# Second chunk of a Fourier-mixing kernel: half of it by plain sums, half by seven products

## The chip, the cores and the metric

One core of one Trainium2 chip. The metric is the device time of one execution in microseconds (us), as the median of several runs. The engines are named as in the profile: PE is TensorE's matmul, PEld its weight load, DVE VectorE, ACT ScalarE, POOL GpSimd, SP SyncE, whose queue issues most of the DMAs.

## The reference

`x` has 2048 tokens of 512 values, all in float32. Of its normalized rows a two-dimensional Fourier transform is taken (real part) and multiplied by a gate from a two-layer network:

```
xn = layernorm(x)
a  = xn @ hid_re.T ;  b = xn @ hid_im.T                # 2048 x 512
s  = seq_re @ a - seq_im @ b                           # 2048 x 2048 matrices
h  = relu(xn @ w1 + b1)**2                             # 2048 x 1792
out = x + s * silu(h @ w2 + b2)
```

The kernel takes the transform along the sequence first, `PQ = [seq_im; seq_re] @ xn`, and the one along the hidden dimension after it.

## The kernel before, in words

**Operands.** Each float32 operand is split into a HI and a LO part (`split`: a copy with rounding on ACT, `split_hi`, line 136, and a subtraction on DVE, `split_lo`, line 139). A product is three matmul passes, HI x HI, HI x LO and LO x HI (`PASSES`).

**The sequence transform.** Its output is cut into `NC` = 8 chunks of `CW` = 256 rows. The sum over 2048 tokens is cut into `NJ` = 8 pairs `j` (128 tokens of the first half of the sequence and 128 of the second). `XC[j]` holds pair j of xn as the stationary operand, in seven slots of two parts: the four raw quarters A11, A21, A12, A22 and the sums S1 to S4, where S1 shares a slot with A21. The slots are HI and LO parts of what lies in `xn32`, which shares buffers `wd0` and `wd1` with the prepared weights. A step (c, j) loads a 512 KB frame `u` of the Fourier matrix (three buffers), forms four more quarters of it (`step_sums`: three DVE operations, lines 304 to 306), splits seven quarters into an operand `g` (`step_split`; two buffers, `ga` for even j and `gb` for odd j) and multiplies.

- *Plain* chunks (0 and 1, `PLAIN` = 2): each pair takes 24 matmuls of 128 x 512 (`one_product`, line 397), into four PSUM banks (`accs`). Only the raw quarters are split, 1024 columns (`plain_parts`). Chunk 0 is accompanied by the layer norm.
- *Seven-product* chunks (2 to 7): Strassen-Winograd products, 7 x 6 = 42 matmuls of 128 x 256 a step (`mm`, line 382), into seven banks, `ms[k]`. The chunk's four quarters are combined from the seven banks at its end (`closing_of`: copies on ACT, seven DVE operations), two of them at once and the rest spread over the next chunk's steps by the table `LATER`, then stored to `PQD[c]` in DRAM.

**Work beside chunk 1.** A chain `aside` is drawn on while chunk 1's products run, with a budget a step (`beside`): `sums(g)` forms S1 to S4 of four pairs in four DVE operations of 1024 columns, S1 in a tile of its own; `split_sums(j)` splits S2 to S4 into `XC[j]`, `split_s1(j)` splits S1 after pair j's last plain product; then the jobs `d0` and `d1`. The frame of chunk 2's first steps is prepared at its end.

**The weights' jobs.** `weight` is a generator of four stages: load the raw weight; form sums (DVE, and for `d` one ACT copy); split and store three slots; split and store four. `d0` to `d3` make the hidden transform's weights (`WDD`), `v0`, `v1`, `v6` three of w1's. They use buffer `pq00`/`pq01` for raw and sums and `wd0` or `wd1` for the parts. The table `EARLY` names after which step which job advances by one stage; `p` loads prepared weights back, `y` prepares what follows.

**Order.** Everything is in program order on each engine, written out by hand. In each iteration of the loop over `steps`: the products of step n, `step_sums(n + 2)`, `step_split(n + 1)`, `step_load(n + 4)`, closing operations, and the jobs of `EARLY`.

**Afterwards.** The hidden transform (`YUnit`, lines 790 on) and the first layer (`HUnit`, 28 units) run as units of seven products; a unit's stages c11, c22, c21, c12 and square run in the midst of the next unit. For units in `ACT_PAIR` both lower quarters get their relu and square on ACT (lines 848 and 879), with plain DVE operations before (lines 800 and 803); for others DVE adds the bias and does relu and square of the lower quarters (lines 860 and 875) and ACT squares half as much. Each unit's region B starts as a negated copy of A (`seed`, line 794). The second layer (`outer`, line 896) ends the kernel.

Of the kernel before, what the change touches and what calls it, by code (L numbers as in the profile page):

```python
# [11 lines left out]
ALU = mybir.AluOpType  # L12
# [10 lines left out]
PLAIN = 2  # L23

ASIDE = 3.6

SIDE = {7: 1}
# [22 lines left out]
LATER = {0: 1, 1: 1, 2: 2, 4: 1}  # L50

# [43 lines left out]
ACT_PAIR = (4, 5, 6, 8, 10, 12, 14, 16, 18, 21, 25)  # L95
# [9 lines left out]
A11, A21, A12, A22, S2, S3, S4 = range(7)  # L105
S1 = A21

# [23 lines left out]
def fnet_gated_kernel(ctx, tc, x, xt, ct, wd, w1, w2, b1, b2, out):  # L131
# [122 lines left out]

    def ln_hi(j, h):

        nc.vector.tensor_scalar(XC[j][:, 2 * h:2 * h + 2, HI, :], halves(xr[j][:, h]), stats[:, 0, h, j:j + 1],
                                stats[:, 1, h, j:j + 1], op0=ALU.subtract, op1=ALU.mult)

    def xc_parts(j, h):  # L260
        s = slice(2 * h, 2 * h + 2)
        return XC[j][:, s, HI, :], XC[j][:, s, LO, :], halves(xn32[j][:, h])

    s1 = {}

    def sums(g):


        s = xn32[ND * g, "tile"].rearrange("p j h (b n) -> p j (h b) n", b=2)
        t = s1[g] = buf(f"pq1{g}", [P, ND, CW], f"s1_{g}")  # L270
        for to, a, b, op in ((t, s[:, :, 1], s[:, :, 3], ALU.subtract),
                             (s[:, :, 1], s[:, :, 1], s[:, :, 0], ALU.subtract),
                             (s[:, :, 0], t, s[:, :, 0], ALU.subtract),
                             (s[:, :, 2], s[:, :, 2], s[:, :, 0], ALU.add)):
            nc.vector.tensor_tensor(to, a, b, op=op)
            yield 1.2

    def split_sums(j):
        s = xn32[j].rearrange("p h (b n) -> p (h b) n", b=2)
        split(XC[j][:, S2:S4 + 1, HI, :], XC[j][:, S2:S4 + 1, LO, :], s[:, 0:3])  # L280
        return 0.9

    def split_s1(j):
        split(XC[j][:, S1, HI, :], XC[j][:, S1, LO, :], s1[j // ND][:, j % ND])
        return 0.4
# [9 lines left out]
    def plain_parts(c, j, hs=slice(0, 2)):  # L295
        if (c, j) not in part:
            part[c, j] = operand_buf("g" + "ab"[j % 2], f"g{c}_{j}", 0 if (c, j) == (PLAIN - 1, NJ - 1) else 3 if j in TURNED else 1, (2, 4, CW))
# [57 lines left out]
    def closing_of(part_, ms, room):  # L355
# [4 lines left out]
        for to, m, frm, op in ((C11, 2, C21, ALU.add), (C22, 6, C21, ALU.add), (C21, 7, C22, ALU.subtract),  # L360
                               (C12, 5, C22, ALU.subtract), (C22, 5, C21, ALU.add), (C12, 3, C12, ALU.add),
                               (C21, 4, C21, ALU.subtract)):
# [10 lines left out]
    def some(steps_, n):  # L373
        for _ in range(n):
            next(steps_)

# [9 lines left out]
    accs = [[bank(tag, f"pq0_{tag}") for tag in ("b20", "b21", "bb", "bc")]]  # L386

    def products(c, j, h):

        for passes in [PASSES] if c else [[q] for q in PASSES]:  # L390
            for k in range(ND):
                one_product(c, j, h, k, passes)

    def one_product(c, j, h, k, passes=PASSES):
        for a_, b_ in passes:
            w = XC[j][:, 2 * h + k // 2, a_, k % 2 * P:(k % 2 + 1) * P]
            nc.tensor.matmul(accs[c][k], w, part[c, j][:, b_, 2 * h:2 * h + 2],  # L397
                             start=j == 0 and h == 0 and (a_, b_) == (HI, HI),
# [832 lines left out]
```

## Time and profile before

| | us |
|---|---|
| median of 3 runs (lowest to highest) | 673.12 (672.95 to 673.25) |
| the profiled execution, its own time | 672.81 |
| its span, first to last instruction | 671.0 |
| PE busy | 665.1 |
| DVE busy | 596.4 |
| ACT busy | 380.2 |
| chunk 1's first matmul starts | 50.95 |
| chunk 2's first matmul starts | 94.67 |
| the hidden transform's first matmul starts | 323.16 |

Times in the profile count from the span's start. Rows in order of time read: start, duration, engine, line, operation, output <- inputs, shapes, count, and in brackets the engine's idle time before it with what ended it. Rows by group have count, busy time, mean duration in ns, idle time before them. A duration is longer than the distance to the next start where operations overlap in an engine's pipeline.

### The profile page before, as it was taken

The page shows a single profiled execution, that of the slowest core. Times are in us where ns is not written, and L with a number is a line of the kernel's source. Part 1 is how long each engine was busy: PE and PEld are TensorE (multiplying, and loading weights), DVE is VectorE, ACT ScalarE, POOL GpSimd, SP SyncE. Part 2 cuts the span into 40 slices and gives each one's busy share as a digit, 9 for nine tenths or more (in the row PEclk, how much of TensorE's full clock was granted, in tenths as well). Part 3 has the DMA queues.
Part 4 walks back from the last instruction along what each step waited for, and adds up shares of the span by engine and source line. Part 5 has one row for each costly group of instructions (what it writes and reads, how often), then busy time and mean ns, then how long its engine had stood idle before and what let it go on. Part 6 is the DMA issues. An engine that isn't in the chain of part 4 may idle for free.

```text
span 671.0 us, 13184 instructions
## 1 busy us (share of the span) xinstructions
PE 665.1 (99%) x5437; PEld 646.3 (96%) x5437; DVE 596.4 (89%) x831; ACT 380.2 (57%) x524; POOL 8.8 (1%) x11
## 2 busy tenths in 40 slices
PE   9999999999999999999999999999999999999997
PEld 6888889999999999999999999999999999999997
DVE  7997888999999999899899988977877889999997
ACT  6855664634445454444464557888778865454451
POOL 0000000000000000000000000000000000101010
PEclk9999999999999999999999999999999999999999
DMA  8635497646556774759588558565755866777775
GB/s 292 226 115 206 145 347 269 220 142 224 200 167 226 252 282 162 262 186 346 184 303 278 181 189 317 202 251 205 271 182 198 324 243 214 190 218 190 219 205 156
DMA packets 51739, 150.82 MB, mean 225 GB/s; under 512 B 4960, under 2 KB 19552, under 8 KB 50272
## 3 DMA queue, kind: packets, MB, share of 16 engines
q1 hardware_dynamic: 43568, 129.28, 56.9%
q10 hardware_dynamic: 6208, 18.88, 7.1%
q0 software_dynamic: 1904, 1.84, 1.9%
q8 instruction: 42, 0.69, 0.4%
q14 instruction: 17, 0.14, 0.1%
HBM read 101.98 MB, written 47.99 MB: 223 GB/s over the span
## 4 chain that ended last, share of the span: by engine, by line
PE 96%; DVE 1%; ACT 1%; DMA 0%; issue 0%; ACTq 0%; SPq 0%; DVEq 0%
PE m L382 34%; PE m_o L896 15%; PE r_B L790 13%; PE r_A L790 9%; PE pq_b L397 8%; PE r_C L790 4%; PE r_D L790 4%; PE m_last L896 4%; PE pq_ba L397 2%; PE pq_bc L397 2%; PE pq_bb L397 2%; DVE z L1146 0%; DMA x<-in_x 0%; DVE z L946 0%; ACT h L848 0%
## 5 line engine op out<-in xcount | busy, mean ns | idle before, releaser
L382 PEld LDWEIGHTS m<-g,xc 128*128 128x128 f32 x2016 | 228.6, 188 | 0.1
L382 PE MATMUL m<-g,xc 128*128 128x256 f32 x2016 | 228.7, 276 | 0.0
L136 ACT ACTIVATE g<-u 128x1792 fp32r<-128x1792 f32 (+2 forms) x65 | 99.0, 1523 | 126.9 <-PE m L382 89.0
L139 DVE TENSOR_TENSOR g<-u,g 128x1792 fp32r<-128x1792 f32 (+2 forms) x66 | 116.9, 1772 | 19.8 <-ACT g L136 19.2
L896 PE MATMUL m_o<-w,g 128*128 128x256 f32 x882 | 100.5, 276 | 0.0
L896 PEld LDWEIGHTS m_o<-w,g 128*128 128x128 f32 x882 | 100.3, 188 | 0.0
L136 ACT ACTIVATE g<-hr 128x1792 fp32r<-128x1792 f32 (+2 forms) x31 | 48.2, 1565 | 40.0 <-PE m_o L896 16.8
L790 PE MATMUL r_B<-xT,w 128*128 128x256 f32 x504 | 66.6, 277 | 0.4 <-ACT r_B L146 0.4
L397 PE MATMUL pq_b<-g,xc 128*128 128x512 f32 x240 | 65.2, 391 | 0.4 <-DVE small L247 0.4
L790 PEld LDWEIGHTS r_B<-xT,w 128*128 128x128 f32 x504 | 61.5, 188 | 0.5 <-ACT r_B L146 0.5
L139 DVE TENSOR_TENSOR g<-hr,g 128x1792 fp32r<-128x1792 f32 (+2 forms) x31 | 56.7, 1837 | 2.9 <-ACT g L136 2.8
L397 PEld LDWEIGHTS pq_b<-g,xc 128*128 128x128 f32 x240 | 44.7, 188 | 10.7 <-ACT g L136 0.8
L790 PE MATMUL r_A<-xT,w 128*128 128x256 f32 x336 | 42.8, 276 | 0.0
L790 PEld LDWEIGHTS r_A<-xT,w 128*128 128x128 f32 x336 | 40.2, 188 | 0.0
L790 PE MATMUL r_B<-wdp,yg 128*128 128x256 f32 x288 | 35.8, 277 | 0.0
L304 DVE TENSOR_TENSOR u<-u 128x512 f32<-128x512 f32 x48 | 32.8, 684 | 1.9 <-DMA u<-in_ct 1.9
L790 PEld LDWEIGHTS r_B<-wdp,yg 128*128 128x128 f32 x288 | 34.1, 188 | 0.0
L896 PE MATMUL m_last<-w,g 128*128 128x256 f32 x294 | 33.5, 276 | 0.0
L896 PEld LDWEIGHTS m_last<-w,g 128*128 128x128 f32 x294 | 33.4, 188 | 0.0
L139 DVE TENSOR_TENSOR yg<-yraw,yg 128x1792 fp32r<-128x1792 f32 x13 | 26.2, 2018 | 0.6 <-ACT yg L136 0.6
L136 ACT ACTIVATE yg<-yraw 128x1792 fp32r<-128x1792 f32 x13 | 22.2, 1708 | 5.8 <-DVE yraw L313 5.3
L790 PE MATMUL r_D<-xT,w 128*128 128x256 f32 x168 | 23.6, 276 | 0.0
(192 smaller groups left out, 877.8 us busy)
## 6 DMA issues: line engine op xcount, KB each, us to landing
u<-in_ct SPq DMA_DIRECT2D x63, 512.0 KB, 3.8
hd<-h ACTq DMA_DIRECT2D x28, 512.0 KB, 3.9
hr<-hd SPq DMA_DIRECT2D x28, 512.0 KB, 3.8
wdp<-wdd SPq DMA_DIRECT2D x8, 896.0 KB, 6.5
yraw<-pqd SPq DMA_DIRECT2D x13, 512.0 KB, 5.9
pqd<-c SPq DMA_DIRECT2D x6, 1024.0 KB, 6.3
w<-w1d SPq DMA_DIRECT2D x6, 896.0 KB, 8.2
y<-y ACTq DMA_DIRECT2D x8, 512.0 KB, 5.2
```

The lines of the kernel that those rows point to most:

```text
L136: nc.scalar.activation(hi, src, AF.Copy)
L139: nc.vector.tensor_tensor(lo, src, hi.bitcast(F32), op=ALU.subtract)
L304: nc.vector.tensor_tensor(t[:, 0:2], r[:, 0:1].to_broadcast([P, 2, 256]), r[:, 1:3], op=ALU.add)
L382: nc.tensor.matmul(ps[:, d], w[:, a_, d * P:(d + 1) * P], halves(mv(b_)), start=first and d == 0 and (a_, b_) == (HI, HI), stop=last and ( ...
L397: nc.tensor.matmul(accs[c][k], w, part[c, j][:, b_, 2 * h:2 * h + 2], start=j == 0 and h == 0 and (a_, b_) == (HI, HI), stop=j == NJ - 1 a ...
L790: nc.tensor.matmul(self.region(REGION[k]), w, mv, start=i == 0 and k in (1, 7), stop=i == len(ops) - 1, skip_group_check=True)
L896: nc.tensor.matmul(m[:, i * 256:(i + 1) * 256], ready[n][:, a_, H_SLOT[a], i * P:(i + 1) * P], W2[p][:, b_, b], start=p == 0 and i == 0 an ...
```

## The change

Chunk 1 becomes mixed. It takes pairs 4 to 7 first (`MIXED`), plain, as four sums of 128 x 256 matmuls through `mm` (`plain_step`): three of the sums go into the banks of products 2, 4 and 3, the fourth into a bank `Z`. Then pairs 0 to 3 follow as seven-product steps into the same banks, as the first four entries of `steps`. Its closing has one DVE operation more where Z's quarter is added, and `LATER_1` spreads it. The slots of `XC` are in another order, so that S2, S3, S4 and S1 lie side by side: `sums` works in place, and `split_sums` splits all four in one operation of 1024 columns on each engine. The chain `aside` is gone: sums and splits stand at fixed places, and the jobs d0 and d1 move into `EARLY`, which shifts those behind them. d1 uses the same raw buffers as the others. Chunk 0's banks change, `junk` has another bank, `g` of chunk 1 has another address offset (`operand_buf`'s step 0), and unit 5 leaves `ACT_PAIR`. The core of the diff:

```diff
-PLAIN = 2
-ASIDE = 3.6
-SIDE = {7: 1}
+MIXED = 4, 5, 6, 7
 EARLY = {
-    (2, 0): ("d2",), (2, 1): ("d2",), (2, 2): ("d3",), (2, 4): ("d3",), (2, 5): ("d3",), (2, 6): ("d3",),
-    (3, 1): ("v0",), (3, 3): ("v0",), (3, 5): ("v0",), (3, 6): ("v0",),
-    (4, 1): ("v1",), (4, 3): ("v1",), (4, 5): ("v1",), (4, 6): ("v1",),
-    (5, 1): ("v6",), (5, 2): ("p1",), (5, 3): ("v6", "p1"), (5, 5): ("v6",), (5, 6): ("v6",),
-    (6, 1): ("y1",), (6, 3): ("y1", "p0"), (6, 6): ("p0",),
+    (1, 0): ("d0",), (1, 2): ("d0",), (1, 3): ("d0",), (2, 0): ("d0", "d1"), (2, 3): ("d1",), (2, 5): ("d1",),
+    (2, 6): ("d1", "d2"), (3, 0): ("d2",), (3, 1): ("d2",), (3, 3): ("d2", "d3"), (3, 5): ("d3",), (4, 0): ("d3",),
+    (4, 1): ("d3", "v0"), (4, 3): ("v0",), (4, 5): ("v0",), (4, 6): ("v0", "v1"), (5, 0): ("v1",), (5, 1): ("v1",),
+    (5, 2): ("p1",), (5, 3): ("v1", "v6", "p1"), (5, 5): ("v6",), (5, 6): ("v6",),
+    (6, 0): ("v6",), (6, 1): ("y1",), (6, 3): ("y1", "p0"), (6, 6): ("p0",),
...
 LATER = {0: 1, 1: 1, 2: 2, 4: 1}
+LATER_1 = {0: 1, 1: 1, 2: 2, 3: 1, 4: 1}
-ACT_PAIR = (4, 5, 6, 8, 10, 12, 14, 16, 18, 21, 25)
+ACT_PAIR = (4, 6, 8, 10, 12, 14, 16, 18, 21, 25)
-A11, A21, A12, A22, S2, S3, S4 = range(7)
+A11, A12, A22, S2, S3, S4, A21 = range(7)
 S1 = A21
...
-        for to, a, b, op in ((t, s[:, :, 1], s[:, :, 3], ALU.subtract),
...
+        for to, a, b, op in ((3, 1, 3, ALU.subtract), (1, 1, 0, ALU.subtract), (0, 3, 0, ALU.subtract), (2, 2, 0, ALU.add)):
+            nc.vector.tensor_tensor(s[:, :, to], s[:, :, a], s[:, :, b], op=op)
...
-        split(XC[j][:, S2:S4 + 1, HI, :], XC[j][:, S2:S4 + 1, LO, :], s[:, 0:3])
-    def split_s1(j):
-        split(XC[j][:, S1, HI, :], XC[j][:, S1, LO, :], s1[j // ND][:, j % ND])
+        split(XC[j][:, S2:S1 + 1, HI, :], XC[j][:, S2:S1 + 1, LO, :], s)
...
+    def plain_step(j):
+        g = part.pop((1, j))
+        for k, pairs_ in ((2, ((A11, 1), (A12, 3))), (4, ((A21, 1), (A22, 3))), (3, ((A11, 0), (A12, 2))),
+                          (Z, ((A21, 0), (A22, 2)))):
+            if k not in ms:
+                ms[k] = bank("ba" if k == Z else banks(1)[k], f"m{k}_1")
+            for i, (a, q) in enumerate(pairs_):
+                mm(ms[k], XC[j][:, a], lambda b_: g[:, b_, q], j == MIXED[0] and not i, k == Z and j == MIXED[-1] and i == 1)
...
-    steps = [(c, j) for c in range(PLAIN, NC) for j in range(NJ)]
-    order = [(c, j) for c in range(PLAIN) for j in range(NJ)] + steps
+    steps = [(1, j) for j in range(NJ) if j not in MIXED] + [(c, j) for c in range(2, NC) for j in range(NJ)]
+    order = [(0, j) for j in range(NJ)] + [(1, j) for j in MIXED] + steps
...
+    for i, j in enumerate(MIXED):
+        if i == 0:
+            some(side[0], 3)
+            split(*plain_parts(1, MIXED[1]))
+            plain_out(0)
+            plain_out(1)
+            split_sums(0)
+            split_sums(1)
+            plain_out(2)
+            plain_out(3)
+            for k in range(2):
+                nc.sync.dma_start(PQD[0][:, k].rearrange("p k n -> p (k n)"), plain[k])
+        elif i == 1:
+            some(side[1], 1)
+            split(*plain_parts(1, MIXED[2]))
+            some(side[1], 1)
+            split_sums(2)
+            split_sums(3)
+        elif i == 2:
+            split(*plain_parts(1, MIXED[3]))
+            some(side[1], 2)
             step_sums(0)
+        else:
+            step_sums(1)
+            step_split(0)
+            split_sums(MIXED[0])
+            split_sums(MIXED[1])
+        plain_step(j)
+        load_c(*order[NJ + i + 4])
...
+        step_sums(n + 2)
+        step_split(n + 1)
+        if n < 2:
+            split_sums(MIXED[n + 2])
+        if n == 0:
+            e = buf("e", [P, 2048], "c1")
+            copy(chunk_part(e)(C22), halves(ms[Z]))
         step_load(n + 4)
```

More of the change, by code (lines that the diff above doesn't have):

```diff
@@ L353, in combine, with closing_of @@
             yield
[L355 removed]
+    def closing_of(part_, ms, room, z):
         copy(part_(C21), halves(ms[1]))
@@ L527, in fnet_gated_kernel @@
     for h in range(2):
-        products(0, 0, h)
-    def run(*names):
-        go(*names)
-        return 1.6
-    aside = chain(sums(0), (split_sums(j) for j in range(ND)), sums(1), (split_sums(j) for j in range(ND, NJ)),
-                  (run(v) for v in ("d0", "d0", "d0", "d1", "d1", "d1")))
+        products(0, h)
+    side = sums(0), sums(1)
     load_c(0, 3)
@@ L564, in fnet_gated_kernel @@
         split_lo(*xc_parts(j, 1))
-        for _ in range(SIDE.get(j, 0)):
-            next(aside)
+        if j == NJ - 1:
+            next(side[0])
         for h in range(2):
-            products(0, j, h)
+            products(j, h)
         g = plain_parts(*order[j + 1])
@@ L630, in fnet_gated_kernel @@
+    LAST = {(c, max(j for c_, j in steps if c_ == c)) for c in range(1, NC)}
     closing = None
```

143 lines of the change are left out of this document (49 added, 94 removed).

## The prediction

> **What bounds the kernel now.** I read the page's busy times first, then the order of time of TensorE, then the stretches by stage, then VectorE's order of time.
>
> ```profile
> PE 665.1 (99%) x5437; PEld 646.3 (96%) x5437; DVE 596.4 (89%) x831; ACT 380.2 (57%) x524; POOL 8.8 (1%) x11
> PE 96%; DVE 1%; ACT 1%; DMA 0%; issue 0%; ACTq 0%; SPq 0%; DVEq 0%
> core 0: us, PE busy (x) PEld busy (x) DVE busy (x) ACT busy (x) POOL busy (x), PEclk, DMA share, GB/s
> 51.10:94.83 43.73, 43.73 (x195) 36.06 (x194) 36.87 (x48) 25.62 (x37) 0.00 (x0) 1.00 0.63 230
> 132.91:171.00 38.09, 38.09 (x339) 38.09 (x338) 35.39 (x45) 17.61 (x14) 0.00 (x0) 1.00 0.57 202
> ```
>
> TensorE is the chain (96%) at clock 1.00 and never idles in the stages that change, so its matmul time counts one for one. But VectorE is 35.4 of 38.1 us busy in a chunk of seven products: little room for more.
>
> **The matmuls.** TensorE in order of time:
>
> ```profile
> 50.95 2.20 PE L397 MATMUL pq_b<-g,xc 128*128 128x512 f32 x9
> 89.07 0.86 PE L397 MATMUL pq_b<-g,xc 128*128 128x512 f32 x3
> 94.67 1.53 PE L382 MATMUL m<-g,xc 128*128 128x256 f32 x12
> 323.16 1.52 PE L790 MATMUL r_A<-wdp,yg 128*128 128x256 f32 x12
> L382 PE MATMUL m<-g,xc 128*128 128x256 f32 x2016 | 228.7, 276 | 0.0
> ```
>
> Chunk 1 has 8 pairs x 24 matmuls of 512 columns: 94.67 - 50.95 = 43.72 us for 192, 227.7 ns each. The seven products: 323.16 - 94.67 = 228.49 us for 2016 of 256 columns, 113.34 ns each, 4.76 us a step of 42. After: four plain steps of 4 sums x 2 x 6 = 48 (5.44 us) and four of 42, 360 x 113.34 = 40.80 us. Saved: **2.92 us**. The unseen price is a plain product in the 256-column form. Low end: 113.34, the same shape and helper with the same address offset of its moving operand. High end: the last pair of chunk 1, the only plain one with that offset, 94.67 - 89.07 = 5.60 us for 24, or 116.7 ns per 256 columns, +0.64 us over 192. I take the low end: shape and offset both agree.
>
> The Trainium skill (TensorE: Matmul & The Clock Gate, section "Wait — 56ns, not 53.3ns?") gives a warm start-to-start of N / 2.4 GHz plus about 2.5 ns, so that halving a matmul costs. By it (an estimate) the chunk would go from 192 x 215.8 = 41.4 to 360 x 109.2 = 39.3 us, a gain of 2.1. The rows differ: two of 256 take 226.7 ns against 227.7 for one of 512, and the trace decides.
>
> **VectorE's room.** A bare step, and the queue's pitch (start to start, shorter than the durations) of what is put into it:
>
> ```profile
> 109.21 1.71 ACT L136 ACTIVATE g<-u 128x1792 fp32r<-128x1792 f32 x1 [3.05 <-PE m L382]
> 110.95 2.02 DVE L139 TENSOR_TENSOR g<-u,g 128x1792 fp32r<-128x1792 f32 x1 [1.21 <-ACT g L136]
> 112.89 0.69 DVE L304 TENSOR_TENSOR u<-u 128x512 f32<-128x512 f32 x1
> 113.61 0.42 DVE L305 TENSOR_TENSOR u<-u 128x256 f32<-128x256 f32 x1
> 114.07 0.42 DVE L306 TENSOR_TENSOR u<-u 128x256 f32<-128x256 f32 x1
> 118.73 1.71 ACT L136 ACTIVATE g<-u 128x1792 fp32r<-128x1792 f32 x1 [2.54 <-issue]
> 120.79 2.02 DVE L139 TENSOR_TENSOR g<-u,g 128x1792 fp32r<-128x1792 f32 x1
> 136.69 0.69 DVE L363 TENSOR_TENSOR c<-left,c 128x512 f32<-128x512 f32 x1
> 137.29 0.68 DVE L304 TENSOR_TENSOR u<-u 128x512 f32<-128x512 f32 x1
> 150.97 0.68 DVE L310 TENSOR_TENSOR w10t<-w10r 128x512 f32<-128x512 f32 x1
> 152.49 0.68 DVE L304 TENSOR_TENSOR u<-u 128x512 f32<-128x512 f32 x1
> 160.50 0.95 DVE L139 TENSOR_TENSOR w10g<-w10r,w10g 128x768 fp32r<-128x768 f32 x1
> 161.36 0.68 DVE L304 TENSOR_TENSOR u<-u 128x512 f32<-128x512 f32 x1
> 165.25 1.22 DVE L139 TENSOR_TENSOR w10g<-w10t,w10g 128x1024 fp32r<-128x1024 f32 x1
> 166.39 0.68 DVE L304 TENSOR_TENSOR u<-u 128x512 f32<-128x512 f32 x1
> 47.95 1.22 DVE L275 TENSOR_TENSOR xn<-xn 128x1024 f32<-128x1024 f32 x1
> 49.20 1.22 DVE L275 TENSOR_TENSOR xn<-s,xn 128x1024 f32<-128x1024 f32 x1
> ```
>
> So: LO split of a step 1.94, three sums 1.52 (the last leaves after 0.34 where the next doesn't need it), a closing operation 0.60, a weight job's sums 1.52, its splits 0.86 and 1.14, an operation of `sums` 1.14, or 1.25 where it needs the one before. A bare step takes 3.46 of 4.76: room 1.30 (the row at 110.95 waited 1.21 for ScalarE). The step's HI split starts 0.26 us after the boundary (94.67 + 3 x 4.76 = 108.95 against 109.21), when TensorE gives its buffer free, and LO follows 1.74 later and takes 2.03; the next step's second matmul wants it 4.76 + 0.11 after the boundary. So VectorE may be about 0.8 us late before TensorE waits.
>
> **VectorE in chunk 1, after.** TensorE's boundaries would be 50.95, 56.39, 61.83, 67.27, 72.71, then by 4.76. Until 62 VectorE keeps up (12 operations of 1.14 to 1.25 since 47.95, with waits for HI). The HI split of pair (1,7) starts at 61.83 + 0.26 = 62.09, takes 1.06 as the rows of that shape do (83.83 below), LO at 63.19. In a row: that 1.14, two of `sums` 1.25 + 1.14, sums of (1,0) and (1,1) 3.04: 69.76; the HI split of (1,0) waits for its sums (68.32), ends at 70.07, LO at 70.11.
>
> ```profile
> 83.83 1.06 ACT L136 ACTIVATE g<-u 128x1024 fp32r<-128x1024 f32 x1 [2.67 <-PE pq_ba L397]
> ```
>
> Behind that waiting HI split on ScalarE stand the parts of pairs 4 and 5, which nothing needs before (1,0) has reached their step; its LO half stands ahead of everything on VectorE.
>
> - (1,1): LO 1.94, parts of pairs 4 and 5 2.28, sums 1.52: LO starts 75.85, lands 77.93 (2.03 and a handover estimated at 0.05; from HI to LO above it is 0.03, 110.92 to 110.95); wanted at 77.58: **0.35 late**.
> - (1,2), (1,3): from 75.85 steps of 4.60 (1.94 + 1.14 + 1.52): on time. (2,0): 85.05 + 1.94 + d0's sums 1.52 + 1.52 = 90.03, lands 92.1: on time (TensorE at 92.10).
> - (2,1): 1.94, two closing 1.20, d0's split 0.87, sums 1.52: starts 95.56, lands 97.64, wanted at 96.97: **0.67 late**. (2,2): 1.94, closing 0.60, d0's split 1.14, sums 1.52: 100.76, lands 102.84: **0.44 late**. Then lateness shrinks.
> - Chunks 3 to 5 use the lateness rule, extras less 1.30 a step: at (3,0) and (5,0) 0.60 + 1.52 leave 0.82, at the next step 0.60 + 0.87 leave 0.99: **0.2 late** in each of the two. Jobs in chunk 4 never add up so.
>
> Sum: **+1.86 us** of waits; low end 0 (room that I miss), high end 2.9 (each handover 0.08 slower, which repeats the waits of chunks 2 to 5).
>
> **The unit taken out of ACT_PAIR.** Unit 5's relu and square halve on ScalarE:
>
> ```profile
> 421.29 0.63 ACT L879 ACTIVATE h<-h 128x512 f32<-128x512 f32 x1
> 431.37 0.73 ACT L848 ACTIVATE h<-h,b1s 128x512 f32<-128x512 f32 x1
> 432.13 1.06 ACT L879 ACTIVATE h<-h 128x1024 f32<-128x1024 f32 x1
> 433.60 0.37 ACT L146 ACTIVATE r_B<-r_A 128x256 f32<-128x256 f32 x1 [0.40 <-ACT h L879]
> 432.82 0.84 PE L790 MATMUL r_D<-xT,w 128*128 128x256 f32 x6
> 434.02 1.66 PE L790 MATMUL r_B<-xT,w 128*128 128x256 f32 x12 [0.35 <-ACT r_B L146]
> 418.17 0.48 DVE L860 SCALAR_TENSOR_TENSOR h<-r_B,b1s,h 128x256 f32<-128x256 f32 x1
> 419.88 0.68 DVE L304 TENSOR_TENSOR xs<-xr 128x512 f32<-128x512 f32 x1
> 428.71 0.42 DVE L800 TENSOR_TENSOR h<-r_B,h 128x256 f32<-128x256 f32 x1
> 429.65 0.96 DVE L139 TENSOR_TENSOR xT<-xr,xT 128x768 fp32r<-128x768 f32 x1
> ```
>
> TensorE was due at 432.82 + 6 x 0.113 = 433.50 and came at 434.02: 0.52 lost to the seed. Without the relu of 0.73 and with the square at 0.63, as the earlier unit's row has it, the seed starts about 1.1 earlier, and that wait goes. VectorE takes over: the earlier unit's lower halves held it from 418.17 to 419.88, 1.71 us, unit 5's from 428.71 to 429.65, 0.94, so the split at 429.65 lands at 431.4 instead of 430.6, some 0.1 behind the matmul that wants it (unit 7's second token half). Net **-0.4** (ends -0.5 and +0.3).
>
> **Moved at no cost.** The plain sums lie in four banks that chunk 0 leaves free, so the copies of chunk 0's banks stand beside 5.44 us steps; without that cover they would cost 4 x 0.6. Slots, strided parts and one split of 1024 for 768 and 256 change names, not lengths. ScalarE (17.6 of 38.1) takes chunk 1's copies. On SP the stores of PQD[0] stand ahead of the load of (1,0): issued near 57.5, wanted at 66.7. The jobs' DMAs are as many as before, later; a v1 split now follows v0's store on the same buffer by three steps: the store goes 5 us after the boundary, the split comes at 16, and the slowest such store took 9.0:
>
> ```profile
> wdd<-wd0g SPq DMA_DIRECT2D x1, 1024.0 KB, 9.0
> DVE u L304 <- DMA u<-in_ct: 1.9, 2, 1.2
> ```
>
> **Sum.** -2.92 + 1.86 - 0.4 = -1.5. The profiled execution took 672.81 (span 671.0), 0.31 under the median 673.12, so 671.3 there and **671.6** as a median. A measurement here tells 0.2% (1.35 us) from no change, so the bound lies at 671.77.
>
> **Rivals.**
> - All of the saving stays: VectorE's lateness never reaches TensorE. For it: no wait in chunks 2 to 7 before. Against: the largest lateness there was 0.35 (HI ended at 118.73 + 1.71, LO started at 120.79, where job d3 stood ahead), so the tolerance was never tried. 673.12 - 3.3 = 669.8. Chance 0.15.
> - No change that can be told: plain products at the 116.7 ns of pair (1,7), or waits at their high end: -1.5 + 0.64 to + 1.05, 672.3 to 672.7. Chance 0.30.
> - Slower: the frames `u` land late. Two such waits of up to 1.2 us stand in the row above and cost nothing, as VectorE had room; with that room spent on jobs in chunks 2 to 5, each delays LO. It decides from three or more such waits (over 2.85 us): about 674.7. Against: each step's load goes out when VectorE is done with the step three before, a full step ahead of its sums. Chance 0.08.
> - The forecast: 0.47, own range 670.8 to 672.2; about seven tenths of it lies below 671.77.
>
> Faster 0.15 + 0.33 = 0.48; same 0.30 + 0.14 = 0.44; slower 0.08. The range 670.0 to 673.1 leaves out the far half of the first rival and the last.
>
> **What would show it.** TensorE: the first of chunk 2's matmuls near 92.1 instead of 94.67, 113.3 ns pitch in the plain steps; waits of TensorE for VectorE's g of 0.3 to 0.7 us at (1,1), (2,1) and (2,2); the first Y matmul near 322.1 instead of 323.16; no wait for the seed near 433. Wrong if VectorE has gaps between 63 and 103 (a DMA or ScalarE is late, or there is room that I missed), or if plain steps exceed 5.5 us.

## The result and the profile after

The change made the kernel slower: 677.56 us as the median of six runs (676.52 to 679.92), against 673.16 (672.95 to 674.04) for the kernel before on the same chip, a ratio of 1.0066 with a 95% interval of 1.0049 to 1.0083. The profiled execution took 676.52 us (span 674.7), against 672.81 for the one before: 3.71 us more. It is the fastest of the six, so the rows below account for that difference and not for all of the median's. One execution of x16 below, of 738.82 us at a granted clock of 0.85 throughout, is left out of every figure.

The busy times of the page after, its chain of waits by engine, and its groups of the seven-product matmuls and of the first of the three sums:

```profile
PE 666.7 (99%) x5605; PEld 654.0 (97%) x5605; DVE 609.1 (90%) x844; ACT 381.8 (57%) x516; POOL 8.8 (1%) x11
PE 89%; DVE 7%; DMA 2%; issue 1%; ACT 1%; SPq 0%; DVEq 0%
...
L376 PE MATMUL m<-g,xc 128*128 128x256 f32 x2376 | 274.0, 278 | 1.7 <-DVE g L138 1.7
...
L296 DVE TENSOR_TENSOR u<-u 128x512 f32<-128x512 f32 x52 | 35.5, 683 | 4.4 <-DMA u<-in_ct 4.3
```

TensorE has fallen from 96% to 89% of the chain and VectorE risen from 1% to 7%, DMA from 0% to 2%. TensorE now idles for VectorE's `g`, and VectorE for a DMA of the frame `u`. TensorE in order of time (start, duration, and in brackets the idle time ahead with what ended it):

```profile
51.42 47.06 PE L376 MATMUL m<-g,xc 128*128 128x256 f32 x403
98.79 11.38 PE L376 MATMUL m<-g,xc 128*128 128x256 f32 x94 [0.32 <-DVE g L138]
109.78 134.87 PE L376 MATMUL m<-g,xc 128*128 128x256 f32 x1168
245.99 81.13 PE L376 MATMUL m<-g,xc 128*128 128x256 f32 x713 [1.34 <-DVE g L138]
326.95 1.52 PE L779 MATMUL r_A<-wdp,yg 128*128 128x256 f32 x12
```

A wait of 0.32 at 98.79 and one of 1.34 at 245.99 show by themselves; smaller ones hide in the long rows, because the modelled ends overlap. So the starts of all 2376 matmuls were taken from the trace, step by step, and set against 113.35 ns from start to start: a single long distance is a wait, and a whole step of 116 to 120 ns distances is a slow pitch. The stretches show that slow pitch as well (us, then busy time and count of TensorE, its weight loads, VectorE, ScalarE and GpSimd, the granted clock, DMA share, GB/s; a matmul that reaches over the edge is counted in):

```profile
core 0: us, PE busy (x) PEld busy (x) DVE busy (x) ACT busy (x) POOL busy (x), PEclk, DMA share, GB/s
51.42:74.02 22.60, 22.60 (x193) 22.60 (x192) 19.54 (x20) 12.52 (x14) 0.00 (x0) 1.00 0.34 117
152.35:182.02 29.67, 29.67 (x254) 29.67 (x253) 27.24 (x35) 14.82 (x13) 0.00 (x0) 1.00 0.65 222
98.20:103.72 5.52, 5.20 (x44) 5.01 (x43) 5.45 (x7) 1.70 (x1) 0.00 (x0) 1.00 0.75 262
```

The four plain steps took 22.60 us for 192 matmuls, 117.7 ns each, without idling, at clock 1.00. Six steps of chunks 3 and 4 took 29.67 for 252, 117.7 again, where the kernel before needed 113.3. Step (2,1) in the last row holds a wait: TensorE is busy for 5.20 of 5.52.

The longest wait, at (5,7), comes from VectorE and from the transfers issued on SP's queue. VectorE in order of time around it:

```profile
239.96 0.43 DVE L305 TENSOR_TENSOR w16t<-w16r,w16t 128x256 f32<-128x256 f32 x1
242.39 0.69 DVE L296 TENSOR_TENSOR u<-u 128x512 f32<-128x512 f32 x1 [2.00 <-DMA u<-in_ct]
243.12 0.42 DVE L297 TENSOR_TENSOR u<-u 128x256 f32<-128x256 f32 x1
243.57 0.42 DVE L298 TENSOR_TENSOR u<-u 128x256 f32<-128x256 f32 x1
243.92 2.02 DVE L138 TENSOR_TENSOR g<-u,g 128x1792 fp32r<-128x1792 f32 x1
```

And SP's queue in order of time before it (start and length of the issuing):

```profile
229.80 0.33 SPq L285 DMA_DIRECT2D u<-in_ct  x1
230.93 0.52 SPq L435 DMA_DIRECT2D w1d<-w11g  x1
231.50 0.72 SPq L426 DMA_DIRECT2D w16r<-in_w  x1
232.27 1.33 SPq L482 DMA_DIRECT2D wdp<-wdd  x1
234.39 0.57 SPq L285 DMA_DIRECT2D u<-in_ct  x1
```

VectorE stood for 2.00 us on a frame whose load went out at 234.39 behind a store of job v1, the raw load of v6 and half of `p1`'s loads. It landed 8.0 us later (242.39 - 234.39), where the median frame takes 3.9. The step's LO split, in front of which the sums stand in program order, therefore came at 243.92 and landed at 245.94; TensorE went on at 245.99.

Where the 3.71 us between the two profiled executions came from (before to after, us):

| stretch | predicted | measured |
|---|---|---|
| start of chunk 1's first matmul, 50.95 to 51.42 | 0 | +0.47 |
| chunk 1, 43.72 to 42.02 (51.42 to 93.44) | -2.92 + 0.35 | -1.70 |
| chunks 2 to 7: waits of LO, VectorE's own lateness | +1.51 | +1.65 |
| chunks 2 to 7: the wait at (5,7) for the frame | 0 | +1.61 |
| chunks 2 to 7: steps at the slow pitch | 0 | +1.74 |
| from the hidden transform's first matmul to the end, 347.87 to 347.79 | -0.4 | -0.08 |

The waits of the third row are 0.59, 0.26 and 0.11 at (2,1), (2,2), (2,5), 0.27 and 0.15 at (3,2), (3,3), 0.12 and 0.15 at (5,2), (5,3). With the two rows under it and 0.02 of rest they are the 5.02 us by which chunks 2 to 7 grew (228.49 to 233.51). In the traces of six kernels below with the same table of jobs the loss at (5,7) is larger: 1.94 to 2.24 us in x9, x10 and x13, and 4.14 to 4.23 in x1, x4 and x5, where the clock was at half behind the wait. So the slower executions of the change probably lost more there too; no trace of one shows it.

### The profile page after: what moved, and what is told of

It reads as the page before. It is cut to its first block, busy times and chain, and to the rows that moved or that the text cites. A ratio compares the mean times of both kernels' runs of the same rounds, so it can differ in the third digit from the quotient of the medians.

```text
span 674.7 us, 13521 instructions
## 1 busy us (share of the span) xinstructions
PE 666.7 (99%) x5605; PEld 654.0 (97%) x5605; DVE 609.1 (90%) x844; ACT 381.8 (57%) x516; POOL 8.8 (1%) x11
## 4 chain that ended last, share of the span: by engine, by line
PE 89%; DVE 7%; DMA 2%; issue 1%; ACT 1%; SPq 0%; DVEq 0%
PE m L376 33%; PE m_o L885 15%; PE r_B L779 13%; PE r_A L779 9%; PE pq_b L387 5%; PE r_C L779 4%; PE r_D L779 4%; PE m_last L885 4%; DVE g L138 2%; PE pq_bb L387 2%; DMA pqd<-c 1%; DMA u<-in_ct 1%; DVE u L296 1%; DVE c L361 1%; DVE z L1135 0%
## 5 line engine op out<-in xcount | busy, mean ns | idle before, releaser
L376 PE MATMUL m<-g,xc 128*128 128x256 f32 x2376 | 274.0, 278 | 1.7 <-DVE g L138 1.7
L376 PEld LDWEIGHTS m<-g,xc 128*128 128x128 f32 x2376 | 273.0, 188 | 2.7 <-DVE g L138 2.4
L135 ACT ACTIVATE g<-u 128x1792 fp32r<-128x1792 f32 (+2 forms) x65 | 101.5, 1562 | 134.9 <-PE m L376 97.0
L138 DVE TENSOR_TENSOR g<-u,g 128x1792 fp32r<-128x1792 f32 (+2 forms) x66 | 120.0, 1818 | 8.6 <-ACT g L135 8.4
L387 PE MATMUL pq_b<-g,xc 128*128 128x512 f32 x144 | 41.3, 393 | 1.2 <-DVE small L246 1.0
L296 DVE TENSOR_TENSOR u<-u 128x512 f32<-128x512 f32 x52 | 35.5, 683 | 4.4 <-DMA u<-in_ct 4.3
L387 PEld LDWEIGHTS pq_b<-g,xc 128*128 128x128 f32 x144 | 26.6, 188 | 8.1 <-ACT g L135 1.4
L297 DVE TENSOR_TENSOR u<-u 128x256 f32<-128x256 f32 x52 | 22.1, 425 | 1.8
```

What stands on the lines that cost most here:

```text
L135: nc.scalar.activation(hi, src, AF.Copy)
L138: nc.vector.tensor_tensor(lo, src, hi.bitcast(F32), op=ALU.subtract)
L296: nc.vector.tensor_tensor(t[:, 0:2], r[:, 0:1].to_broadcast([P, 2, 256]), r[:, 1:3], op=ALU.add)
L297: nc.vector.tensor_tensor(t[:, 2], t[:, 1], r[:, 1], op=ALU.add)
L376: nc.tensor.matmul(ps[:, d], w[:, a_, d * P:(d + 1) * P], halves(mv(b_)), start=first and d == 0 and (a_, b_) == (HI, HI), stop=last and ( ...
L387: nc.tensor.matmul(accs[k], w, part[0, j][:, b_, 2 * h:2 * h + 2], start=j == 0 and h == 0 and (a_, b_) == (HI, HI), stop=j == NJ - 1 and ...
```

## The experiments

The numbers in the labels give the order in which they ran. A ratio is to the kernel before, with its 95% interval. "Slow pitch" and "waits" are sums over the steps of the sequence transform as above, of the profiled execution. That one can lie well off the median: 673.20 in x3, 676.03 in x11, 675.92 in x13, 678.00 in x14. Diffs are against the changed kernel where nothing else is said.

### Why a plain product costs 117.7 ns

**x1.** The moving operand of chunk 1's plain steps gets chunk 0's address steps (1 or 3, of 16 columns each) in place of 0:

```diff
-... operand_buf("g" + "ab"[j % 2], f"g{c}_{j}", 0 if c else 3 if j in TURNED else 1, (2, 4, CW))
+... operand_buf("g" + "ab"[j % 2], f"g{c}_{j}", 3 if j in TURNED else 1, (2, 4, CW))
```

> The changed kernel with the plain operands of pairs 4 to 7 at the address offset that chunk 0's have, and nothing else. Theory (address): TensorE's slow pitch of 117.8 ns in the plain steps and in (1,0) and (1,1) (51.4 to 83.9) comes from that offset; expected 113.4 ns there, 5.44 us a plain step. VectorE's chain then sets the end of chunk 2's first steps, so only some 0.4 to 1.2 of the 1.2 us come back: 676.3 to 677.1 against 677.56. Rival (form): 256-column plain products are slow in themselves, whatever the offset; then 117.8 stays and the time is unchanged.

678.24 us (677.58 to 678.92, 4 runs), ratio 1.007 (1.0055 to 1.0085). The stretch of the four plain steps:

```profile
50.75:73.76 23.01, 23.01 (x193) 23.01 (x192) 19.73 (x21) 12.51 (x14) 0.00 (x0) 1.00 0.35 117
```

23.01 us for 192 is 119.8 ns: slower still, where 113.4 was expected. But the slow pitch ended with the plain steps; (1,0) and (1,1) ran at 113.4 here, and at 117.8 in the changed kernel. The offset alone isn't it.

**x5.** The same operand as a [128, 2, 7, 256] tile, as the seven-product steps have it, HI and LO 1792 columns apart:

```diff
+            if c:
+                part[c, j] = buf("g" + "ab"[j % 2], [P, 2, 7, CW], f"g{c}_{j}", F32R)
```

> The changed kernel with the plain operands of pairs 4 to 7 laid out as those of the seven products are: 1792 columns, not 1024, between HI and LO, no offset. Theory (address): the pitch of a plain step depends on where HI and LO lie, since another offset has already changed it (117.8 to 120 ns); expected 113.4 in the plain steps and in (1,0) and (1,1), chunk 2 near 92.4. VectorE's chain then takes most of it back at (2,1) and (2,2): 676.5 to 677.5. Rival (the stationary side or the form): 117 to 120 ns stay.

679.16 us (678.59 to 679.68, 4 runs), ratio 1.0087 (1.0072 to 1.0102). The pitch stayed at 117.8 in the plain steps and in (1,0), (1,1). The distance between HI and LO isn't it either. Much of what x1 and x5 lie above their expected times is at (5,7), where their profiles lost 4.23 and 4.14 us, with the clock at half for 3.41.

**x9 and x10.** Address steps 2 and 3 in every plain step of chunk 1, a single run each:

```diff
-... 0 if c else 3 if j in TURNED else 1 ...
+... 2 if c else 3 if j in TURNED else 1 ...      # x9
+... 3 if c or j in TURNED else 1 ...             # x10
```

> The changed kernel with the plain operands of pairs 4 to 7 two address steps (128 bytes) off instead of none. Theory (address): some offset gives 113.4 ns in the plain steps; this one or three steps off does. Rival (form): 117 to 120 ns at each offset.

> The same with three address steps off. Theory (address): 113.4 ns here or at two steps. Rival (form): 117 to 120 ns.

677.74 and 676.83 us. Step 2 gave 117.8 ns with the carry into (1,0) and (1,1), like 0; step 3 gave 120 without the carry, like x1. No address step of these operands, 0 to 3, brings 113.3.

**x6.** The kernel *before*, with the one exception in its plain operands taken out, which gave its last pair (1,7) address step 0:

```diff
-... 0 if (c, j) == (PLAIN - 1, NJ - 1) else 3 if j in TURNED else 1 ...
+... 3 if j in TURNED else 1 ...
```

> The kernel before with pair (1,7)'s operand at the address offset of its neighbours. Theory (address): its 24 matmuls take 226.7 ns each instead of 233.3, chunk 2 starts 0.16 us earlier, and nothing else moves: 673.0. Rival: 233 ns stay, the pitch belongs to the order of that pair's sums (two banks first).

673.54 us, a single run. Pair (1,7) lost its high price (226.7 ns a matmul of 512 columns in place of 233), and the slow pitch appeared behind it, in a kernel that had none. The stretches of three steps from chunk 2's start, and of four from there:

```profile
95.04:109.67 14.63, 14.63 (x127) 14.63 (x126) 13.47 (x17) 7.39 (x7) 0.00 (x0) 1.00 0.84 303
109.69:128.72 19.03, 19.03 (x171) 19.03 (x169) 16.73 (x22) 9.02 (x7) 0.00 (x0) 1.00 0.56 185
```

By the starts, (2,0) and (2,1) took 4.947 and 4.944 us (95.03, 99.97, 104.92) and (2,2) 4.76; from there on four steps take 19.03, 4.76 each. So the slow pitch isn't a property of the plain product. It is a state that TensorE enters where matmuls of 512 columns give way to 256, keeps without idling, and leaves later; a last 512-column pair at address step 0 avoids it, at 233 ns a matmul. One thing isn't parted: in x6, as in the change, the moving operand's address step goes from 1 to 0 at the same matmul as the columns from 512 to 256. In x1 it stays at 1 there and the steps are slow all the same, at 120, so that change isn't needed for a slow pitch; no run has the one without the other at 117.8.

**x13.** Hence the same exception put into the changed kernel, for chunk 0's last pair:

```diff
-... 0 if c else 3 if j in TURNED else 1 ...
+... 0 if c or j == NJ - 1 else 3 if j in TURNED else 1 ...
```

> The changed kernel with the operand of chunk 0's last pair (0,7) at the offset that the plain operands of chunk 1 have, as the kernel before does with (1,7). Theory (a state entered at the change of form, left by a pair at another offset): (0,7) takes 233 ns a matmul, 0.16 us more, and the plain steps, (1,0) and (1,1) then run at 113.4: chunk 2 1.0 us earlier; VectorE takes most of it back at (1,1), (2,1) and (2,2), so 676.8 to 677.5. Rival (the form): 117.8 stays in the plain steps and (0,7) costs 0.16.

678.22 us (675.92 to 678.94, 4 runs), ratio 1.007 (1.0054 to 1.0086). The plain steps:

```profile
51.24:72.99 21.75, 21.75 (x193) 21.75 (x192) 18.93 (x20) 12.53 (x14) 0.00 (x0) 1.00 0.36 121
```

21.77 us from 51.23 to 73.00 for 192, 113.4 ns: the price that the prediction took, reached by a change outside the plain steps (x14, x15 and x17, with the same exception, have it too). The median didn't move; the profiled execution, of 675.92, is the fastest of the four. With TensorE on time, VectorE is late where the prediction had it (0.52 at (1,1), 0.59 at (2,1), 0.26 at (2,2)), and the waits grew to 4.0 us, with 1.94 at (5,7). A faster pitch alone only moves the loss.

### Whether a wait by itself sets off the slow pitch

**x12.** The kernel *before*, with `step_sums` run three times instead of once at four places, which delays the next LO:

```diff
+            if s in ((3, 0), (4, 2), (5, 4), (6, 5)):
+                step_sums(n + 2)
+                step_sums(n + 2)
```

> The kernel before with step_sums called three times instead of once at (3,0), (4,2), (5,4) and (6,5), the same result each time: 3.0 us more on VectorE, so that its LO split is late and TensorE waits about 1 to 2 us once at each. Theory (a wait sets off the slow pitch): after some of the four waits 117.8 ns for a step or more, and never before them. Rival (chance, or the changed kernel's own layout): 113.4 all through.

686.39 us, a single run. TensorE lost 3.84, 1.65, 4.17 and 1.87 us at (3,1), (4,3), (5,5) and (6,6). The stretches around the first: the idle time with its end, the 3.4 us behind it, two steps, one step:

```profile
138.06:140.30 2.24, 0.28 (x3) 0.08 (x1) 2.24 (x3) 1.70 (x1) 0.00 (x0) 1.00 0.00 0
140.31:143.71 3.40, 3.40 (x16) 3.40 (x17) 3.33 (x5) 0.00 (x0) 0.00 (x0) 0.52 0.46 154
146.78:156.66 9.88, 9.88 (x86) 9.88 (x85) 7.60 (x9) 3.41 (x2) 0.00 (x0) 1.00 0.34 122
156.68:161.42 4.74, 4.74 (x44) 4.74 (x43) 4.64 (x8) 1.71 (x1) 0.00 (x0) 1.00 0.34 111
```

Two things follow an idle time of 2 us here. The granted clock falls to 0.52 for the next 3.40 us, which takes twice the time of the same work; and once it is back at 1.00, two steps run at 9.88 / 84 = 117.6 ns before (3,4) is at 4.76 again. Behind the wait at (5,5) it was the same, with four slow steps. The two shorter waits halved no clock; behind the one at (4,3) the rest of its own step was slow (0.17 us), behind the one at (6,6) nothing. So a wait can set off both, and need not.

### The late frame and VectorE's room

**x2.** `p1`'s two loads go out earlier, after (4,2) and (4,4):

```diff
-    (5, 2): ("p1",), (5, 3): ("v1", "v6", "p1"), ...
+    (4, 2): ("p1",), ..., (4, 4): ("p1",), ..., (5, 3): ("v1", "v6"), ...
```

> The changed kernel with the two loads of job p1 moved from after (5,2) and (5,3) to after (4,2) and (4,4). Theory (queue): the 1.6 us wait at step (5,7) comes from step (5,3), where v1's store, v6's raw weight and half of p1 stand ahead of the load of a frame; with p1 away the frame lands in time, the wait goes, and the time falls by 1.3 to 1.6. Rival (VectorE alone): the lateness of VectorE makes that wait, the frame's landing is only last by a little; then it falls by less than 0.5, or a wait of the same kind comes up in chunk 4.

677.74 us (676.21 to 679.41, 5 runs), ratio 1.0064 (1.0043 to 1.0085). The wait at (5,7) fell from 1.61 to 0.25, so `p1`'s transfers were its cause. The time stayed. VectorE's waits, of this kernel:

```profile
DVE g L138 <- ACT g L135: 10.6, 17, 2.4
DVE u L296 <- DMA u<-in_ct: 6.1, 5, 1.5
```

Five late frames and 6.1 us (four of them of 1.20 to 1.51, at 129, 207, 266 and 280 us) in place of three and 4.3: new waits of TensorE came at (3,0), (5,0), (5,2) and (6,4), 0.42 to 0.79 each. The frames at 129, 207 and 266 stand ahead of three of them; behind the one at 280 TensorE waited for nothing.

**x3.** The jobs' sums and LO parts become copies on ScalarE, so VectorE gets its room back; what they compute is left out:

```diff
-        sums_(t, r)
+        copy(t, r)
...
-            split(g[:, HI, q], g[:, LO, q], src)
+            split_hi(g[:, HI, q], g[:, LO, q], src)
+            split_hi(g[:, LO, q], g[:, HI, q], src)
```

> The changed kernel with the weights' jobs d and v taken off VectorE: their sums and LO parts are plain copies on ScalarE, so what they compute is left out; DMAs and order as they were. Frees about 3.5 us of VectorE a job, 24.7 us in all. Theory (room): the waits at (2,1), (2,2), (2,5), (3,2), (3,3), (5,2), (5,3), some 1.9 us, go, and with them the slow pitch after them in (2,1), (3,4) to (4,1) and (5,3), some 1.6 us, which a wait sets off; the wait at (5,7) shrinks as VectorE has room for a late frame: 672.5 to 674. The slow pitch from 51.4 to 83.9 stays. Rival (slow pitch independent of waits): only the waits go, 117.8 ns still stands in (3,4) to (4,1): 675 to 676.

675.08 us (672.91 to 677.61, 10 runs), ratio 1.0019 (1.0004 to 1.0035). TensorE's waits fell to 1.81 us, 0.88 of it at (5,7), and the slow pitch of chunks 2 to 5 to 0.17, at (2,1). The 1.23 of chunk 1 stayed. That is the profiled execution, one of the fastest; they spread over 4.7 us, and the median lies above the theory's 672.5 to 674, in the rival's range by time though not by pitch.

**x7.** The same operations on GpSimd:

```diff
-        sums_(t, r)
+        sums_(t, r, nc.gpsimd)
...
-            split(g[:, HI, q], g[:, LO, q], src)
+            split_hi(g[:, HI, q], g[:, LO, q], src)
+            nc.gpsimd.tensor_tensor(g[:, LO, q], src, g[:, HI, q].bitcast(F32), op=ALU.subtract)
```

> The changed kernel with the sums and LO parts of the jobs d and v on GpSimd, which is idle in these chunks; all is computed. Theory (room): as with the jobs off VectorE, the waits from (2,2) to (5,3) go: 674 to 676. Rival (GpSimd disturbs VectorE, or is so slow that the jobs' stores and buffers are late): VectorE's operations take longer or ScalarE stands waiting for a buffer, 677 or more.

692.18 us (691.05 to 694.81, 4 runs), ratio 1.0286 (1.0259 to 1.0313): 19 us of waits. That is the rival's case. A split of 1024 columns, 1.22 on VectorE, takes GpSimd 2.6 to 4.2; the one of job v0:

```profile
L435 POOL TENSOR_TENSOR w10g<-w10t,w10g 128x1024 fp32r<-128x1024 f32 x1 | 3.6, 3628 | 2.0 <-ACT w10g L135 2.0
```

**x8.** x2 and x3 together:

> Both of two earlier edits: the jobs' sums and LO parts as copies on ScalarE (what they compute is left out), and p1's loads after (4,2) and (4,4). Theory (two causes, VectorE's room and the queue at (5,3)): no wait is left but the one at (2,1) that ScalarE's copies make, only the slow pitch of 51 to 83; 672 to 673. Rival (frames land late wherever jobs' transfers stand, the place is chance): waits of 0.5 to 1 us come up elsewhere and the median stays near 675.

673.16 us (671.88 to 673.97, 10 runs), ratio 0.9992 (0.9983 to 1.0002). One wait is left in the sequence transform, 0.53 at (2,1); another, of 0.81, came in the hidden transform (at 368.46). VectorE's waits, of this kernel:

```profile
DVE g L138 <- ACT g L135: 25.6, 36, 2.4
DVE u L296 <- DMA u<-in_ct: 9.9, 10, 1.9
```

Ten frames came late, 9.9 us in all, more than twice what the changed kernel shows, and TensorE lost no more than 0.1 us behind any of them: VectorE, which stood 25.6 us for ScalarE's `g`, had the room. A late frame costs by what VectorE is behind, not by itself. The changed kernel has one of 1.74 at 280.33 that cost nothing either.

**x11.** A whole version: all jobs are spread by a rule that keeps VectorE's forecast lateness low.

```diff
-    (1, 0): ("d0",), (1, 2): ("d0",), (1, 3): ("d0",), (2, 0): ("d0", "d1"), (2, 3): ("d1",), (2, 5): ("d1",),
-    (2, 6): ("d1", "d2"), (3, 0): ("d2",), (3, 1): ("d2",), ...
+    (1, 0): ("d0",), (1, 2): ("d0",), (2, 0): ("d0",), (2, 3): ("d0", "d1"), (2, 5): ("d1",), (2, 6): ("d1",),
+    (3, 0): ("d1", "d2"), (3, 3): ("d2",), (3, 4): ("d2", "d3"), ...
```

> The changed kernel with the same jobs spread otherwise: at most one stage a step and none where the closing takes two, d0's first split after (2,0), the last ones up to (6,3), p1 after (4,7) and (5,2), p0 after (6,6) and (7,0), y1 after (6,3) and (6,5). All is computed. Theory (density): by the lateness rule with 1.30 of room and 0.8 of tolerance no wait is left behind (1,1), nor the slow pitch after one; the slow pitch of 51 to 83 stays: 2.4 us of waits, some 1.5 of pitch less, 672.5 to 674. Rival (VectorE is short over the whole stretch, whatever the order, or frames land late): waits of 1.5 us and more come up at other places, 675 to 677.

674.92 us (674.09 to 676.03, 8 runs), ratio 1.0026 (1.0015 to 1.0036): 2.6 us better than the change. Chunk 2, which had 0.96 us of waits, has none left:

```profile
94.00:130.00 36.00, 36.00 (x320) 36.00 (x319) 34.85 (x47) 17.33 (x14) 0.00 (x0) 1.00 0.64 213
```

318 distances of 113.3 fill the 36.00 us; VectorE is busy for 34.85 of them. But 3.53 us of waits came elsewhere: 1.34 at (4,0) and 1.18 at (6,0), and five of 0.15 to 0.27. Ahead of the two long ones VectorE stood on a job's raw weight: 1.20 us at 167.00, for ScalarE's copy of `wd3r`, which had waited for its load; 0.75 at 244.13 for `w16r`, and 0.47 behind that for a frame. The theory's 672.5 to 674 was missed.

**x14.** x13's exception, with the jobs spread so that each raw load goes out three steps ahead of its sums:

```diff
-    (1, 0): ("d0",), (1, 2): ("d0",), (1, 3): ("d0",), (2, 0): ("d0", "d1"), (2, 3): ("d1",), ...
+    (1, 0): ("d0",), (2, 0): ("d0",), (2, 3): ("d0", "d1"), (2, 5): ("d0",), (2, 6): ("d1",), ...
```

> That, and the jobs spread so that each raw load stands three steps or more ahead of its sums, the lateness rule leaves no wait behind (1,1), and p1 and p0 follow after (4,7), (5,2), (6,7) and (7,0). All is computed. Theory (density and late raw loads): of the first spread's 3.5 us of waits less than 1.5 stay; if the state theory holds too, 672 to 673.5, else 673 to 674.2. Rival (frames land late wherever): as the first spread, 674.5 to 675.5.

674.82 us (674.07 to 678.0, 9 runs), ratio 1.0028 (1.0017 to 1.0038). The waits on raw weights went, and waits on frames took their place. VectorE in order of time, before the wait at (4,2):

```profile
173.57 0.69 DVE L361 TENSOR_TENSOR c<-left,c 128x512 f32<-128x512 f32 x1
175.57 0.69 DVE L296 TENSOR_TENSOR u<-u 128x512 f32<-128x512 f32 x1 [1.31 <-DMA u<-in_ct]
```

TensorE lost 0.48 and 0.81 at (4,2) and (4,3), 1.41 at (7,0). The profiled execution, the slowest of the nine, lost 2.42 more in the hidden transform (at 370.91). The median is in the rival's range, not the theory's.

**x15 and x16.** x14, with the jobs' raw loads, their stores and `p`'s loads issued by GpSimd's queue (x15), and the stores of `PQD` too (x16):

```diff
-        nc.sync.dma_start(r, raw_)
+        nc.gpsimd.dma_start(r, raw_)
...
-            nc.sync.dma_start(t[:, i].bitcast(F32), WDD[n][:, i])
+            nc.gpsimd.dma_start(t[:, i].bitcast(F32), WDD[n][:, i])
```

> The kernel with both edits (last pair's offset, jobs spread), and the jobs' raw loads and stores and p's loads issued on GpSimd's queue instead of SP's. All is computed. Theory (queue order): frames land late because they stand behind the jobs' 0.5 to 1 MB on SP's queue; on another queue VectorE's waits for frames (some 5 us in the sum there) shrink to under 2, 671.5 to 673. Rival (bandwidth): the 16 DMA engines share what both queues want, the frames are as late, 674 to 675.5; or GpSimd's queue makes its descriptors slowly and the jobs themselves come late, more than 675.

> The same with the chunks' own stores of 1 MB on GpSimd's queue too. Theory (queue order): another step in the same direction, 671 to 673. Rival (bandwidth): no difference to the one before within 0.5.

x15: 676.86 us (675.61 to 678.02, 6 runs), ratio 1.0049 (1.0034 to 1.0064), with seven late frames and 5.7 us, against five and 5.2 in x14; the median frame landed in 4.3 us, against 3.7 in x14. x16: 677.10 us (675.60 to 680.97, 5 runs), ratio 1.0062 (1.0038 to 1.0086), without a trace of any of the five; that is within 0.5 of x15, as its rival had it. Another queue for the jobs doesn't bring the frames sooner: standing in line behind them is not what makes the frames late here. The Trainium skill (Trainium Kernel Development and Optimization, section "Key Constraints") says that the queues of SP, ACT and POOL all run on the same 16 DMA engines and that issuing from several saves the sequencer's issue time alone. The traces agree: 3.7 from one queue, 4.3 from two.

### The unit taken out of ACT_PAIR

**x4.** Unit 5 put back:

```diff
-ACT_PAIR = (4, 6, 8, 10, 12, 14, 16, 18, 21, 25)
+ACT_PAIR = (4, 5, 6, 8, 10, 12, 14, 16, 18, 21, 25)
```

> The changed kernel with unit 5 back in ACT_PAIR. Theory: the waits that the changed kernel has near 419 and 435 (0.24 and 0.31 us) give way to the one of the kernel before near 433 to 437 (0.63): within 0.2 us of the changed kernel. Rival: no wait comes, as the units stand later against the loads: 0.5 us less.

679.3 us, a single run, outside the 0.2 that was expected. From the hidden transform's first matmul to the end it took 348.12 us against 347.79, so the edit is worth about 0.3: the wait of 0.63 is back in place of 0.32, and the one of 0.24 near 419 stayed, as 0.22. The 2.4 us by which that run is above the changed kernel's profiled one up to there came earlier, at (5,7): 4.15 us, with the clock at half for 3.41.

### What is left of the saving when both causes go

**x17.** x8 with x13's exception: VectorE has room, `p1` is early, and the plain steps keep the fast pitch.

```diff
-... 0 if c else 3 if j in TURNED else 1 ...
+... 0 if c or j == NJ - 1 else 3 if j in TURNED else 1 ...
```

> Three edits together: the jobs' sums and LO parts as copies on ScalarE (what they compute is left out), p1's loads after (4,2) and (4,4), and (0,7)'s operand at the later pairs' offset. Theory (room, frames and pitch are all that took the saving): against the first two together (673.16) the 1.2 us of slow pitch in chunk 1 go, about 0.2 for (0,7) and its first waits come: 671.7 to 672.5, 0.7 to 1.4 under the kernel before. Rival (something else in the change costs): 673 again.

672.34 us (671.49 to 674.67, 12 runs), ratio 0.999 (0.998 to 0.9999). TensorE in order of time:

```profile
51.01 26.81 PE L376 MATMUL m<-g,xc 128*128 128x256 f32 x235
78.05 19.87 PE L376 MATMUL m<-g,xc 128*128 128x256 f32 x168 [0.24 <-DVE g L138]
98.15 224.37 PE L376 MATMUL m<-g,xc 128*128 128x256 f32 x1973 [0.23 <-DVE g L138]
322.35 1.52 PE L780 MATMUL r_A<-wdp,yg 128*128 128x256 f32 x12
```

The hidden transform starts at 322.35, 0.81 ahead of the kernel before and 4.60 ahead of the change. The prediction had 322.1. From the first plain matmul (51.01 against 50.95) that is 0.87 us gained: 2.92 less 1.28 of waits, at (1,1), (2,1) and (5,0), and 0.78 of slow steps at and behind the first two. The weights' sums are missing in this kernel, so it is no version to use; it shows that the saving is in the matmuls, and that VectorE's room, the frames and the pitch took it. No kernel that does the whole computation beat the one before: the best are x14 and x11, at 674.82 and 674.92.

## Why the prediction was wrong

It said 671.6 and gave a loss a chance of 0.08; the median is 677.56. By its own steps:

- **The matmuls, -2.92 us: right in number, wrong in price.** 360 matmuls replaced 192, as counted. The step that failed is "I take the low end: shape and offset both agree." The plain product cost 117.7 ns, a little over the high end (116.7) that the rival with chance 0.30 had, a plain step 5.65 us where over 5.5 was to show the prediction wrong; and, what the bounds didn't hold at all, the seven-product steps (1,0) and (1,1) behind it ran at the same pitch: 1.23 us gone in chunk 1. No address step or layout of the plain operands brought the fast pitch (x1, x5, x9, x10). What precedes them did (x13, and the other way round x6). The row of pair (1,7) at 89.07, read as the high end of one price, hid that link: with its address step at that of its neighbours the pair is fast and the steps behind it are slow (x6). What the state is, no run here settles.
- **VectorE's room and the lateness rule: right, in place and size.** 1.86 us were forecast at (1,1), (2,1), (2,2) and the starts of chunks 3 and 5; 1.65 came, 0.59 at (2,1) for 0.67. (1,1) had none, because the slow pitch gave VectorE the time; in x13 and x17, at the fast pitch, it came, at 0.52 and 0.51 for 0.35. x11 emptied chunk 2 of waits by the same rule.
- **What a wait leaves behind: missed.** The sum counted a wait as its own length. 1.74 us more came as slow steps in chunks 2 to 5, 1.33 of them from (3,2) to (4,1). With fewer waits all but 0.17 went in x3 (x8 kept two more slow steps behind its wait at (2,1), 0.37); with waits put into the kernel before (x12) they came behind three of four. Against a simple rule: in x4, x5, x9 and x10 a stretch began at (4,5), and in x14 at (5,3), with a wait of 0.02 at most.
- **The frames: the rival with chance 0.08 took part.** "Each step's load goes out when VectorE is done with the step three before, a full step ahead of its sums" is the argument that failed. The load of (5,7) did go out ahead, at 234.39, and needed 8.0 us. Its mechanism held otherwise: three such waits, 4.3 us on VectorE, against two and 1.9 before. In the profiled execution only the one at (5,7) cost TensorE time, 1.61, less than the 2.85 that the rival asked for. It isn't one place that can be cleared (x2, x11, x14, x15); it needs room on VectorE (x8).
- **Unit 5, -0.4: the unit gave -0.3, the stretch -0.08.** The wait of 0.63 for the seed went as said, but 0.24 came at 418.26 and 0.32 at 434.14, where twelve matmuls take longer than the 1.52 of their neighbours. TensorE in order of time, and from the page what its weight loads waited for:

```profile
416.90 0.84 PE L779 MATMUL r_C<-xT,w 128*128 128x256 f32 x6
417.58 0.84 PE L779 MATMUL r_D<-xT,w 128*128 128x256 f32 x6
418.26 1.76 PE L779 MATMUL r_B<-xT,w 128*128 128x256 f32 x12
419.86 1.52 PE L779 MATMUL r_A<-xT,w 128*128 128x256 f32 x12
...
432.78 1.52 PE L779 MATMUL r_B<-xT,w 128*128 128x256 f32 x12
434.14 1.84 PE L779 MATMUL r_A<-xT,w 128*128 128x256 f32 x12
...
L779 PEld LDWEIGHTS r_B<-xT,w 128*128 128x128 f32 x504 | 61.5, 188 | 0.2 <-DVE h L849 0.2
L779 PEld LDWEIGHTS r_A<-xT,w 128*128 128x128 f32 x336 | 40.3, 188 | 0.2 <-DVE xT L138 0.2
```

  The second is the one that the sum had at 0.1: VectorE's split of `xT` for unit 7 is late, and by more than forecast. The first isn't the unit's: with unit 5 put back (x4) it is still there, and x3, x7, x11, x14, x15 and x17, with the unit out, don't have it. There an operation of VectorE that reads `r_B` came at 418.54, behind the sums of a raw weight. Put back, the unit costs 0.33, so sign and size of its term were about right, and what ate it was VectorE's order elsewhere; why VectorE is later at 418 than before was not tested.
- **What was moved at no cost** held: no stall at the plain sums' banks and none of SP's stores in chunk 1.

The differences of the table's rows, +0.47, +0.87, +0.14, +1.61, +1.74 and +0.32, are the 5.15 us between the predicted -1.46 and the measured +3.71, up to 0.02. The first, a later start of chunk 1, isn't the change's as far as can be seen: it varied from 50.6 to 52.1 over these profiles, and was 51.47 and 51.49 in x6 and x12, whose first chunk is that of the kernel before.

## What to carry to other kernels

When TensorE is the chain and the engine that feeds it is over nine tenths busy, a cut in matmuls that pays with feeding work has to be costed against the feeder's room step by step, its late transfers included: a transfer that was late at no cost becomes a wait as soon as the room is spent. Read TensorE's pitch at every change of matmul form and behind every wait in the trace, and not only its mean, and let the sum hold the steps that follow. A version that leaves the suspected work out tells soonest whether the saving is there at all (x8, x17).

## What the runs showed of the hardware

- A stream of 256-column matmuls has more than one steady pitch at clock 1.00: 113.3 ns, and 117.7, or 120 at two address steps of the moving operand. The slower one is entered where 512 columns give way to 256 (x6) or behind a wait (x12), in five traces also with no wait over 0.02 us, lasts for one to seven steps without idling, and ended in most traces behind a pair 1 or 3 of the sequence sum, whose stationary operands lie at another address step than the rest.
- A wait of about 2 us can halve the clock behind it. The trace's clock records give 3.413 us at 0.5 in x1, x4, x5 and x7, and twice in x12. The stretches between the records of x12 are 136.533 and 98.987 us, 40 and 29 times 3.4133. Laid out on that grid, back from the last record of each trace, TensorE's idle time within one stretch of 3.4133 us was 1.97 to 2.87 us in the six that the half clock followed (2.13 in x1, 1.97 in x12), and 1.67 at most in all others between 40 and 660 us. Idle times of 1.96 in x9 and 3.02 in x7 halved nothing: they lie across an edge of the grid, as 0.66 + 1.30 and 1.66 + 1.36. The Trainium skill (TensorE: Matmul & The Clock Gate, Part 1) has the clock gate look at free-running windows of 3413 ns and halve the clock after one idle window or more. The length and the grid agree; that a window must be idle as a whole doesn't, since 1.97 us of idling did it. A mean clock of 0.997 in the changed kernel's slowest run (679.92) fits one such stretch (0.5 x 3.413 / 678 = 0.0025).
